# q's shift row in one fp32r matmul: VectorE folds its halves, and the row is summed one tile later

## The chip, the core and the metric

The kernel runs on one core of one Trainium2 chip. The metric is the device time of one execution in microseconds, the median over several executions. The engines are called here as the profile calls them: PE is TensorE's matmuls, PEld its weight loads, DVE is VectorE, ACT is ScalarE, POOL is GpSimd, and SP issues most DMA transfers.

## The reference, cut to what matters

```python
x = A_x                                             # (1, 2048, 448)
mod = (silu(c) @ w_mod).reshape(c.shape[0], 6, 1, -1)
sa, ca, ga, sb, cb, gb = mod[:, 0] ... mod[:, 5]
h = layernorm(x) * (1 + ca) + sa
x = x + ga * A(h)        # linear attention, 16 heads of 28: q, k, v = h @ wqkv, phi(t) = elu(t) + 1
h = layernorm(x) * (1 + cb) + sb
x = x + gb * B(h)        # mixer MLP over the 2048 tokens: gelu(h^T w1 + b1) w2 + b2
```

The change concerns the first step of the attention. For q, and likewise for k, the kernel needs `(layernorm(x) * (1 + ca) + sa) @ w`. It does not normalise x ahead of the projection. It multiplies x itself with `w' = (1 + ca) w` and adds two rank-one terms: minus the token's mean times the column sums of `w'`, and the token's deviation times the *shift row* `sa @ w`. Both rows, the column sums and the shift row, are computed once for q and once for k.

## The kernel before, in words

**Precision.** The products run in fp32r. To keep fp32's precision, a matrix is split into a high part (a copy rounded to fp32r, made by ACT) and a low part (the rest, made by DVE), and a product takes three matmuls: high by high, high by low, low by high. `hh`, `hl` are the high and low parts of x^T, `wh`, `wl` those of `w'` (j = 0 for q, j = 1 for k), `pkh`, `pkl` those of phi(k), `xh`, `xl` those of the normalised x.

**Stages.** First come the projections and the sums over tokens, up to about 100 us. Then come the attention's output and the two layer norms around it, and from about 150 us on the mixer's two large products. Each engine carries out its instructions in the order in which the code writes them (`tc.manual_schedule()`); the engines wait for each other by semaphores. Tiles come from pools: `slots` with 74 buffers, `tok` with 27 (the smaller pool), and `cst` for constants. A new tile gets a buffer that an earlier one has left, and its first writer waits for that one's last user.

**The loop of the change** is `for t in range(4, NT)`: 16 tiles of 128 tokens. In turn t, PE projects k of tile t+1 (`project(t + 1, 1, "kp")`, ten matmuls), closes tile t with the matmul on the two rows (`close(t, 1)`), and adds tile t-4 to the outer product (`a_outer`, eleven matmuls into `cacc`). In odd turns it also transposes the rows of means and deviations of tiles t+1 and t+2 (`a_transpose`, tile `rw`, from `rowst`; ACT copies them into `hl` of both tiles). In turns 10 to 14 it projects one tile of q as well (`a_q`, `qp`). Meanwhile DVE and ACT make phi(k), normalise, split, and prepare two tiles ahead. POOL computes the powers of the variances and issues transfers that add phi(k) into `pkl` and into the running sums `pk0` and `pk1`.

**The shift row of q (j = 0).** In turns 5 to 8, DVE's `row_part` adds up `accb0`: on each of 128 partitions, the four chunks of w_q, each times the column `sa`. What is left to do is to sum over the partitions. In turn 9, behind `close(9, 1)`, PE does seven fp32r matmuls with `sel_s`, which give minus the column sums of `w'` (`row_sum`), and one with `sel_b` on `accb0`, both plain fp32, which gives the shift row (`row_bias`). All go into one PSUM bank, `rowb0`. At the end of turn 9, `row_out` reads the rows out: ACT writes the high parts into `wrow0`, DVE the low parts. The first q tile closes with `wrow0` in turn 10. The same happens for k (j = 1) ahead of the loop, and stays as it is.

**mod.** The shares of w_mod for ga, cb, sb, gb are summed in the same way by `mod_part` (into `acc2`, `acc4`, ...). `mod_add` folds the upper 48 partitions onto the lower, and `mod_high` splits the sum into 64 partitions of high and 64 of low part (`mh`), so that one fp32r matmul with ones (`mod_sum2`, bank `modp`) sums both.

Of the kernel before, what the change touches and what calls it, by code (L numbers as in the profile page):

```python
# [8 lines left out]
F32 = mybir.dt.float32  # L9
F32R = mybir.dt.float32r  # L10
AF = mybir.ActivationFunctionType
# [3 lines left out]
P = 128  # L15
S, D, F = 2048, 448, 1792
# [15 lines left out]
ROWS = 98  # L32
# [19 lines left out]
def block_kernel(ctx: ExitStack, tc: tile.TileContext, x, xt, wqkv, wo, w1, b1, w2, c, wmod, wfirst, out):  # L52
    nc = tc.nc
# [5 lines left out]
    cst = ctx.enter_context(tc.tile_pool(name="cst", bufs=1))  # L59
# [16 lines left out]
    def moving(new, name, dt=F32R, parts=P):  # L76
        return new(name, dt=dt, parts=parts, w=512)[:, 16:16 + D]
# [22 lines left out]
        nc.gpsimd.affine_select(out=m3, in_=m3, compare_op=ALU.is_ge, fill=0.0, base=DH - 1,  # L100
                                pattern=[[0, 4], [DH, 4], [0, DH]], channel_multiplier=-1)

    cst.tile([P, 112], F32, name="space")
    mhalf = cst.tile([P, 2], F32, name="mhalf")
    nc.vector.memset(mhalf, -0.5)
    roots = cst.tile([P, 2], F32, name="roots")
# [2 lines left out]
    sel_b = cst.tile([P, ROWS], F32, name="sel_b")  # L109
# [3 lines left out]
    for i in (64, 66, 96):  # L113
        nc.gpsimd.memset(sel_f[:, i:i + 1], -1.0)
        nc.gpsimd.memset(sel_b[:, i + 1:i + 2], 1.0)
    sel_s = cst.tile([P, ROWS], F32R, name="sel_s")
    rowst = []
    for i in range(RING):
        rowst.append(cst.tile([P, P], F32R, name=f"rowst{i}"))
# [115 lines left out]
    def mod_add(j):  # L235
        acc = macc[j]
        nc.vector.tensor_add(acc[:G - 64], acc[:G - 64], acc[64:])

    def mod_high(j):
        acc, both = macc[j], moving(slot, f"mh{j}")  # L240
        macc[j] = (both,)
        nc.scalar.activation(both[:64], acc[:64], AF.Copy)
        return lambda: nc.vector.tensor_sub(both[64:], acc[:64], both[:64].bitcast(F32))
# [5 lines left out]
    def mod_sum2(j):  # L249
        ps = bank(f"modp{j}")  # L250
        part = macc.pop(j)
        for i, m in enumerate(part):
            nc.tensor.matmul(ps[:, :D], ones_r[:m.shape[0], :], m, start=(i == 0), stop=(i == len(part) - 1))
        return ps

    Whi, Wlo, Wrow, rowb, accb = {}, {}, {}, {}, {}
# [26 lines left out]
    def row_sum(j):  # L283
        rowb[j] = bank(f"rowb{j}")
        ws = [Whi[j, ch] for ch in range(4)] + [Wlo[j, ch] for ch in range(3)]
        for i, w in enumerate(ws):
            nc.tensor.matmul(rowb[j][:ROWS, :D], sel_s, w, start=(i == 0), stop=False)  # L287

    def row_bias(j):
        nc.tensor.matmul(rowb[j][:ROWS, :D], sel_b, accb.pop(j), start=False, stop=True)  # L290

    def row_out(j):
        ps, w = rowb.pop(j), Wrow[j]
        nc.scalar.activation(w[64:ROWS], ps[64:ROWS, :D], AF.Copy)
        nc.vector.tensor_sub(w[96:ROWS], ps[96:ROWS, :D], w[96:ROWS].bitcast(F32))
# [77 lines left out]
    def a_stats_dve(ts):  # L373
        g, ve = a_group(ts)

        b6 = {}

        def first(i):
            b6[i] = small.tile([P, 6], F32, name=f"st{ts[i]}", tag="st")
            nc.vector.bn_stats(b6[i], X[ts[i]])  # L380

        def second(i):
            nc.vector.bn_aggr(mv[ts[i]][:, 0:2], b6[i])

        def end():
            nc.vector.tensor_scalar_add(ve, g[:, :, 1:2].to_broadcast([P, len(ts), 2]), EPS)
            a_pow(g, ve)
            groups[ts[0]] = g
        return first, second, end
# [11 lines left out]
    def a_transpose(t):  # L401
        ps = bank(f"rw{t}")
        tps[t], tps[t + 1] = ps[:ROWS - 64, :P], ps[64:ROWS, :P]
        nc.tensor.transpose(ps[:ROWS, :P], rowst[t // 2 % RING][:, :ROWS].bitcast(F32), ident)
# [29 lines left out]
    def project(t, j, name):  # L434
        projects([(t, kind, ch) for ch in range(3) for kind in ("hh", "wl", "hl")] + [(t, "hh", 3)], j, name)

    def close(t, j):
        ps = pps.pop((t, j))
        nc.tensor.matmul(ps[:, :D], heads[t][1][:ROWS, 384:], Wrow[j][:ROWS], start=False, stop=True)  # L439
        return ps[:, :D]  # L440
# [3 lines left out]
    def a_exp1(t, ps):  # L444
        eks[t] = (slot(f"ek{t}"), slot(f"rk{t}"))
        nc.scalar.activation(eks[t][0], ps, AF.Exp, scale=mv[t][:, 2:3])

    def a_relu(t, ps):
        nc.scalar.activation(eks[t][1], ps, AF.Relu, scale=mv[t][:, 2:3])

    def a_exp(t, ps):
        a_exp1(t, ps)
        a_relu(t, ps)
# [22 lines left out]
    def a_q(t):  # L476
        project(t, 0, "qp")
        qps[t] = close(t, 0)
        del heads[t]
# [30 lines left out]
    def a_pk(t, ps):  # L510
        pkf[t] = phi_k(t, ps, tslot if t < 2 else slot)
# [33 lines left out]
    def a_outer(t):  # L545
        if not cacc:
            cacc.extend(bank(f"cacc{ch}") for ch in range(4))
        xh, xl = xss.pop(t)
        kh, kl = pks.pop(t)
        for ch in range(4):  # L550
            s = slice(ch * P, (ch + 1) * P)
            todo = [(xh, kh), (xh, kl)] + ([(xl, kh)] if ch < 3 else [])
            for i, (a, b) in enumerate(todo[::1 if t > 1 else 2]):
                nc.tensor.matmul(cacc[ch][:, :D], a[:, s], b, start=(t == 0 and i == 0),  # L554
                                 stop=(t == NT - 1 and i == len(todo) - 1))
        if t < 2:
            for ch in range(4):
                nc.tensor.matmul(cacc[ch][:, :D], xh[:, ch * P:(ch + 1) * P], kl, start=False, stop=False)
# [59 lines left out]
    kps = [close(t, 1) for t in (0, 1)]  # L618
# [63 lines left out]
    for t in range(4, NT):  # L682
        if 5 < t < NT - 1:
            project(t + 1, 1, "kp")
        kp = close(t, 1) if t > 4 else kps[4]
        if t == 9:
            row_sum(0)
            row_bias(0)
        if t > 4:
            a_outer(t - KV_LAG)  # L690
        if t % 2 and 4 < t < NT - 2:
            a_transpose(t + 1)
        if t in Q_EARLY:
            a_q(Q_EARLY[t])
        if t == 12:
            mp = mod_sum2(2)
        pair = t % 2 and 7 < t + 3 < NT
        if pair:
            first, second, end = a_stats_dve((t + 3, t + 4))
            first(0)  # L700
        if 5 <= t < 9:
            w_low(0, t - 5)
        if pair:
            second(0)
        if 5 <= t < 9:
            row_part(0, t - 5)
        a_phi_q(t in Q_EARLY)
        if t == 9:
            a_exp(t, kp)
        if t % 2 and 4 < t < NT - 2:  # L710
            a_copy(t + 1)
            a_copy(t + 2)
        if t != 9:
            a_exp(t, kp)
        if 7 < t + 3 < NT:
            a_split_high(t + 3)
        a_pk_parts(t - 1)
        highs = HIGH_AT.get(t, (t - 2,))
        for i in highs[:1]:
            a_norm(i)  # L720
            a_high(i)
        if t % 2 == 0 and 4 < t < NT - 3:
            low = a_rows(t + 2)
        if t == 11:
            low2 = mod_high(2)
        for j, i in MOD_AT.get(t, ()):
            mod_add(j) if i is None else mod_part(j, i)
        if t == 14:
            low4()
        a_pk(t, kp)  # L730
        if t % 2 == 0 and 4 < t < NT - 3:
            low()
        if 7 < t + 3 < NT:
            a_split_low(t + 3)
        for i in highs[1:]:
            a_norm(i)
            a_high(i)
        if pair:
            first(1)
        for i in highs:  # L740
            a_low(i)
        if pair:
            second(1)
            end()
        sum_end()
        if 4 <= t < 8:
            w_high(0, t - 4)
            if t == 7:
                w_row(0)
        if t == 9:  # L750
            row_out(0)
        if t == 12:
            mod_out(2, mp)
            make_mask()
        if t in FETCH:
            load_xt(FETCH[t])
            load_x(FETCH[t])
        if 7 <= t < 11:
            mod_part(2, t - 7)
        if t == 10:  # L760
            mod_add(2)
        if t == 11:
            low2()
        if t == 13:
            low4 = mod_high(4)
        if t in (7, 10):
            load_mod(4 if t == 7 else 3)
        if t == 10:
            load_qkv(2, tslot)
        if t == 8:  # L770
            for g in range(4):
                w = tslot(f"wo{g}", parts=G)
                nc.sync.dma_start(w, wo[g * G:(g + 1) * G, :])
                wo_sb.append(w)
            b12 = cst.tile([P, NF + NT], F32, name="b12")
            nc.sync.dma_start(b12, b1)
            b1c, b2c = b12[:, :NF], b12[:, NF:]
        if t >= 13:
            nc.vector.tensor_mul(wo_sb[t - 13], wo_sb[t - 13], mods[2][:G])
        load_to(PRE_LOAD.get(t, 0))  # L780
# [34 lines left out]
    for ch in range(4):  # L815
        for g in range(4):
            s = slice(g * G, (g + 1) * G)
            nc.tensor.matmul(kvb[:G, s], raw_w[2, ch][:, s], csum[ch][:, s], start=(ch == 0 and g == 0),  # L818
                             stop=(ch == 3), skip_group_check=True)
# [168 lines left out]
    for i in range(NT + LAG):  # L988
# [11 lines left out]
        t = i - LAG  # L1000
# [292 lines left out]
    for o0, n in W1G[1:]:  # L1293
# [5 lines left out]
        for r in range(first, NT):  # L1299
# [5 lines left out]
            if xleft:  # L1305
                t = xleft.pop(0)
# [80 lines left out]
```

## Time and profile before

| | |
|---|---|
| time, median of 3 runs | 433.37 us (433.19 to 434.04) |
| the profiled execution's own time | 434.09 us |
| its span, first to last instruction | 432.4 us |
| granted TensorE clock | 1.0 |
| busy PE, DVE, ACT, POOL | 427.9, 365.1, 278.9, 120.1 us |
| `rowb` matmuls with `sel_s` (L287), for k and q | 14, each 0.36 us from start to end |
| `rowb` matmuls with `sel_b` (L290), for k and q | 4 records, each 0.54 us from start to end |

Matmuls overlap, so that what one of them takes of PE's path is the distance from its start to the next one's, not its duration. The plain fp32 matmul has two records of its own. In rows of the timeline, an entry in brackets at the end is the idle time of that engine before the instruction, and what ended it. An instruction's number of elements is partitions by elements of a partition.

### The profile page before, as it was taken

The page shows a single profiled execution, that of the slowest core. Times are in us where ns is not written, and L with a number is a line of the kernel's source. Part 1 is how long each engine was busy: PE and PEld are TensorE (multiplying, and loading weights), DVE is VectorE, ACT ScalarE, POOL GpSimd, SP SyncE. Part 2 cuts the span into 40 slices and gives each one's busy share as a digit, 9 for nine tenths or more (in the row PEclk, how much of TensorE's full clock was granted, in tenths as well). Part 3 has the DMA queues.
Part 4 walks back from the last instruction along what each step waited for, and adds up shares of the span by engine and source line. Part 5 has one row for each costly group of instructions (what it writes and reads, how often), then busy time and mean ns, then how long its engine had stood idle before and what let it go on. Part 6 is the DMA issues. An engine that isn't in the chain of part 4 may idle for free.

```text
span 432.4 us, 7216 instructions
## 1 busy us (share of the span) xinstructions
PE 427.9 (99%) x2331; PEld 398.0 (92%) x2331; DVE 365.1 (84%) x814; ACT 278.9 (65%) x595; POOL 120.1 (28%) x199
## 2 busy tenths in 40 slices
PE   8999999999999999999999999999999999999997
PEld 8888899999899999999999999999999999999996
DVE  4899987889899999998579695739799998898894
ACT  5799869658578899996755263537464664655550
POOL 4345444300026577775200000010113131132010
PEclk9999999999999999999999999999999999999999
DMA  8997997565300036354427461577379977986431
GB/s 282 385 337 162 239 264 162 89 206 193 86 1 0 26 74 148 74 125 97 145 85 244 142 212 50 166 203 210 79 193 214 207 159 159 214 170 144 85 46 41
DMA packets 63797, 66.14 MB, mean 153 GB/s; under 512 B 4816, under 2 KB 55312, under 8 KB 63760
## 3 DMA queue, kind: packets, MB, share of 16 engines
q1 hardware_dynamic: 54688, 50.90, 37.8%
q0 software_dynamic: 8784, 14.32, 20.8%
q10 hardware_dynamic: 288, 0.46, 0.4%
q8 instruction: 18, 0.29, 0.3%
q14 instruction: 19, 0.16, 0.1%
HBM read 46.30 MB, written 7.34 MB: 124 GB/s over the span
## 4 chain that ended last, share of the span: by engine, by line
PE 97%; DVE 1%; ACT 1%; issue 0%
PE y L1183 19%; PE up L951 10%; PE up L950 10%; PE up L952 10%; PE y L1184 9%; PE cacc L554 7%; PE qp L432 7%; PE op L893 7%; PE kp L432 6%; PE op L900 1%; PE warm L188 1%; PE tq L863 1%; PE qp L439 1%; PE kvb L818 1%; PE wp L968 1%; PE rowb L287 1%
## 5 line engine op out<-in xcount | busy, mean ns | idle before, releaser
L950 PE MATMUL up<-h2h,ph 128*128 128x448 f32 x224 | 81.2, 362 | 0.0
L951 PE MATMUL up<-h2l,ph 128*128 128x448 f32 x224 | 81.2, 362 | 0.0
L952 PE MATMUL up<-h2h,pl 128*128 128x448 f32 x224 | 80.8, 361 | 0.0
L1138 POOL DMA_DIRECT2D a<-a x16 | 14.2, 964 | 142.6 <-DMA pr<-in_B_w_dram 76.7
L950 PEld LDWEIGHTS up<-h2h,ph 128*128 128x128 f32 x224 | 42.0, 188 | 3.1
L952 PEld LDWEIGHTS up<-h2h,pl 128*128 128x128 f32 x224 | 41.9, 187 | 3.0
L951 PEld LDWEIGHTS up<-h2l,ph 128*128 128x128 f32 x224 | 42.0, 188 | 2.3
L84 DVE TENSOR_TENSOR pl<-pr,ph 128x512 fp32r<-128x512 f32 x46 | 30.7, 688 | 2.6 <-ACT ph L83 1.7
L1189 ACT ACTIVATE cc<-y 128x448 f32<-128x448 f32 x24 | 13.0, 546 | 26.7 <-PE y L1184 26.7
L1102 DVE TENSOR_TENSOR u<-u,mod 128x448 f32<-128x448 f32 x14 | 8.7, 623 | 23.0 <-ACT u L1101 22.8
L83 ACT ACTIVATE ph<-pr 128x512 fp32r<-128x512 f32 x46 | 27.6, 623 | 0.8 <-PE up L952 0.5
L1101 ACT ACTIVATE u<-up,b 128x448 f32<-128x448 f32 x14 | 8.8, 625 | 25.4 <-PE up L952 24.9
L432 PE MATMUL kp<-wh,hh 128*128 128x448 f32 x64 | 23.8, 377 | 0.0
L554 PE MATMUL cacc<-pkh,xh 128*128 128x448 f32 x64 | 23.6, 369 | 0.0
L432 PE MATMUL qp<-wh,hh 128*128 128x448 f32 x64 | 23.5, 368 | 0.0
L1203 POOL DMA_DIRECT2D out_dram<-yt x14 | 12.7, 909 | 37.3 <-DVE yt L1194 27.9
L843 POOL TENSOR_SCALAR den<-den 128x16 f32<-128x16 f32 x16 | 8.8, 548 | 44.2 <-DVE den L840 44.2
L554 PE MATMUL cacc<-pkl,xh 128*128 128x448 f32 x56 | 20.3, 362 | 0.0
L893 PE MATMUL op<-wph,pth 128*128 128x448 f32 x48 | 18.7, 390 | 0.0
L1144 DVE TENSOR_TENSOR a<-a,s 128x512 f32<-128x512 f32 (+1 forms) x32 | 18.5, 622 | 0.0
L83 ACT ACTIVATE s2h<-s 128x512 fp32r<-128x512 f32 (+1 forms) x16 | 8.3, 569 | 15.5 <-DVE s L1144 15.5
L1183 PE MATMUL y<-ub,a11h 128*128 128x448 f32 x56 | 18.2, 375 | 0.0
(235 smaller groups left out, 1383.7 us busy)
## 6 DMA issues: line engine op xcount, KB each, us to landing
pr<-in_B_w_dram SPq DMA_DIRECT2D x56, 256.0 KB, 3.1
a<-in_B_w_dram SPq DMA_DIRECT2D x32, 256.0 KB, 4.8
a<-in_B_w_dram SPq DMA_DIRECT2D x32, 192.0 KB, 4.7
xt<-in_xt_dram SPq DMA_DIRECT2D x16, 256.0 KB, 5.0
x<-in_A_x_dram SPq DMA_DIRECT2D x16, 224.0 KB, 5.0
wm<-in_B_wmod_dram SPq DMA_DIRECT2D x16, 196.0 KB, 5.2
out_dram<-x SPq DMA_DIRECT2D x14, 224.0 KB, 2.3
out_dram<-yt POOLq DMA_DIRECT2D x14, 224.0 KB, 6.1
```

What stands on the lines that cost most here:

```text
L83: nc.scalar.activation(hi, full, AF.Copy)
L84: nc.vector.tensor_sub(lo, full, hi.bitcast(F32))
L432: nc.tensor.matmul(pps[t, j][:, :D], a[:, ch * P:(ch + 1) * P], w, start=first, stop=False)
L554: nc.tensor.matmul(cacc[ch][:, :D], a[:, s], b, start=(t == 0 and i == 0), stop=(t == NT - 1 and i == len(todo) - 1))
L893: nc.tensor.matmul(opb[t][:, :D], a, b, start=(ch == n == 0), stop=False)
L950: nc.tensor.matmul(ps[:, :D], hi[:, sl], mh, start=first, stop=False)
L951: nc.tensor.matmul(ps[:, :D], hi[:, sl], ml, start=False, stop=False)
L952: nc.tensor.matmul(ps[:, :D], lo[:, sl], mh, start=False, stop=last)
L1138: nc.gpsimd.dma_start(w, a, accum_op=ALU.add)
L1144: nc.vector.tensor_tensor(w, raw2[q, a][i], raw2[q, b][i], op=op)
L1183: nc.tensor.matmul(ps[:, :D], h[:, s], w, start=opens and r == 0, stop=False, skip_group_check=True)
L1184: nc.tensor.matmul(ps[:, :HD], l[:, s], wh, start=False, stop=closes and r == PAIRS - 1, skip_group_check=True)
```

## The change

For q alone, the shift row goes the way of the mod shares:

- In turn 8, behind the low part of the rows of tiles 10 and 11, DVE folds the upper half of `accb0` onto the lower (`row_fold`).
- In turn 9, ACT writes the high part of the 64 partitions into a new tile `rb0` of the smaller pool, and a copy of `sel_b` in fp32r, `sel_r`; DVE writes the low part into `rb0`'s other 64 partitions (`row_high`).
- `row_sum` and `row_bias` move from turn 9 to turn 10, behind tile 11's projection. `row_bias` is now one fp32r matmul of `sel_r` on `rb0`.
- `row_out` moves from the end of turn 9 to turn 10, behind `close(10, 1)`.
- `a_exp(9)` comes ahead of the statistics in turn 9.
- `mod_add(2)` moves from the end of turn 10 into turn 11, ahead of `mod_high(2)`.
- A constant that only took up space shrinks by as much as `sel_r` takes.

```diff
-    cst.tile([P, 112], F32, name="space")
+    cst.tile([P, 14], F32, name="space")
...
+    sel_r = cst.tile([P, ROWS], F32R, name="sel_r")
...
     def row_bias(j):
-        nc.tensor.matmul(rowb[j][:ROWS, :D], sel_b, accb.pop(j), start=False, stop=True)
+        nc.tensor.matmul(rowb[j][:ROWS, :D], sel_r if j == 0 else sel_b, accb.pop(j), start=False, stop=True)
+
+    def row_fold(j):
+        acc = accb[j]
+        nc.vector.tensor_add(acc[:64], acc[:64], acc[64:])
+
+    def row_high(j):
+        acc, both = accb[j], moving(tslot, f"rb{j}")
+        nc.scalar.activation(both[:64], acc[:64], AF.Copy)
+        nc.scalar.activation(sel_r, sel_b, AF.Copy)
+        accb[j] = both
+        return lambda: nc.vector.tensor_sub(both[64:], acc[:64], both[:64].bitcast(F32))
...
         if 5 < t < NT - 1:
             project(t + 1, 1, "kp")
-        kp = close(t, 1) if t > 4 else kps[4]
-        if t == 9:
+        if t == 10:
             row_sum(0)
             row_bias(0)
+        kp = close(t, 1) if t > 4 else kps[4]
+        if t == 10:
+            row_out(0)
         if t > 4:
             a_outer(t - KV_LAG)
...
+        if t == 9:
+            a_exp(t, kp)
+            row_high(0)()
         if pair:
             first, second, end = a_stats_dve((t + 3, t + 4))
             first(0)
...
         a_phi_q(t in Q_EARLY)
-        if t == 9:
-            a_exp(t, kp)
...
         if t == 11:
+            mod_add(2)
             low2 = mod_high(2)
...
         if t % 2 == 0 and 4 < t < NT - 3:
             low()
+        if t == 8:
+            row_fold(0)
...
-        if t == 9:
-            row_out(0)
...
-        if t == 10:
-            mod_add(2)
```

The order on PE around turns 9 and 10. Before, behind the closing matmul of tile 9 (the ellipses leave out the row's other matmuls and those of the outer product and the projection):

```order
L439 MATMUL kp9_733<-wrow1_280,hl9_630 128x448
L287 MATMUL rowb0_806<-wh0_0_534,sel_s_100 98x448
...
L290 MATMUL rowb0_806<-accb0_561,sel_b_90 98x448
L554 MATMUL cacc0_437<-pkh5_632,xh5_701 128x448
...
L404 MATMUL rw10_826<-ident_78,rowst2_105 98x128
L432 MATMUL kp11_870<-wh1_0_222,hh11_762 128x448
L432 MATMUL kp11_870<-wl1_0_224,hh11_762 128x448
L432 MATMUL kp11_870<-wh1_0_222,hl11_763 128x448
...
L439 MATMUL kp10_794<-wrow1_280,hl10_692 128x448
```

And now:

```order
L451 MATMUL kp9_734<-wrow1_281,hl9_631 128x448
L566 MATMUL cacc0_438<-pkh5_633,xh5_702 128x448
...
L416 MATMUL rw10_819<-ident_78,rowst2_106 98x128
L444 MATMUL kp11_865<-wh1_0_223,hh11_763 128x448
L444 MATMUL kp11_865<-wl1_0_225,hh11_763 128x448
L444 MATMUL kp11_865<-wh1_0_223,hl11_764 128x448
...
L288 MATMUL rowb0_876<-wh0_0_535,sel_s_100 98x448
...
L291 MATMUL rowb0_876<-rb0_825,sel_r_101 98x448
L451 MATMUL kp10_796<-wrow1_281,hl10_693 128x448
```

The eight matmuls of the row moved behind the outer product of tile 5, the rows of tiles 10 and 11 and the projection of tile 11.

The order on DVE in turns 8 and 9, with the semaphores that an instruction waits for in brackets (`DMAHW` those of SP's transfers, `DMASW` those of POOL's). Before:

```order
L395 CAST rowst2_105<-mv10_677 128x4x2 [waits Pool_49]
L458 SCALAR_TENSOR_TENSOR pk8_776<-ek8_758,rk8_759 128x448 [waits Activation_49]
L398 TENSOR_TENSOR rowst2_105<-mv10_677,rowst2_105 128x2x2 [waits DVE_49]
L415 TENSOR_TENSOR hl11_763<-xt11_536,hh11_762 128x512 [waits DMAHW3_49,Activation_49]
L505 TENSOR_TENSOR xh6_772<-xn6_770,xh6_772 128x64 [waits DMASW6_49,DMASW5_49,Activation_49]
L506 TENSOR_TENSOR xl6_773<-xn6_770,xh6_772 128x384
L232 SCALAR_TENSOR_TENSOR acc2_723<-wm2_1_374,sc_194,acc2_723 112x448 [waits DMAHW6_49]
L380 BN_STATS st12_830<-x12_597 128x6 [waits DMAHW6_49]
```

And now:

```order
L407 CAST rowst2_106<-mv10_678 128x4x2 [waits Pool_49]
L470 SCALAR_TENSOR_TENSOR pk8_777<-ek8_759,rk8_760 128x448 [waits Activation_49]
L410 TENSOR_TENSOR rowst2_106<-mv10_678,rowst2_106 128x2x2 [waits DVE_49]
L295 TENSOR_TENSOR accb0_562<-accb0_562 64x448
L427 TENSOR_TENSOR hl11_764<-xt11_537,hh11_763 128x512 [waits DMAHW3_49,DVE_49,Activation_49]
L517 TENSOR_TENSOR xh6_773<-xn6_771,xh6_773 128x64 [waits DMASW6_49,DMASW5_49,Activation_49]
L518 TENSOR_TENSOR xl6_774<-xn6_771,xh6_773 128x384
L233 SCALAR_TENSOR_TENSOR acc2_724<-wm2_1_375,sc_195,acc2_724 112x448 [waits DMAHW6_49]
L302 TENSOR_TENSOR rb0_825<-accb0_562,rb0_825 64x448 [waits Activation_49]
L392 BN_STATS st12_831<-x12_598 128x6 [waits DMAHW6_49]
```

The fold stands between the rows' low part and hl11, and hl11 has a wait for a semaphore of DVE's own beside the two that it had; rb0's low part follows four instructions on, ahead of the statistics of x12.

The order on DVE in turn 11, around the first writers that wait for the buffer of pk9 (phi(k) of tile 9). Before:

```order
L496 TENSOR_SCALAR xn9_1014<-x9_370,mv8_554 128x448
L230 TENSOR_SCALAR acc4_1021<-wm4_0_725,sc_194 112x448 [waits DMAHW1_49,PE_49]
L232 SCALAR_TENSOR_TENSOR acc4_1021<-wm4_1_727,sc_194,acc4_1021 112x448 [waits DMAHW2_49,DVE_49]
L232 SCALAR_TENSOR_TENSOR acc4_1021<-wm4_2_729,sc_194,acc4_1021 112x448 [waits DVE_49]
L458 SCALAR_TENSOR_TENSOR pk11_1025<-ek11_1002,rk11_1003 128x448 [waits PE_49,Activation_49]
L415 TENSOR_TENSOR hl14_1007<-xt14_865,hh14_1006 128x512 [waits DMAHW2_49,Activation_49]
L380 BN_STATS st15_1028<-x15_932 128x6 [waits DMAHW5_49]
L505 TENSOR_TENSOR xh9_1016<-xn9_1014,xh9_1016 128x64 [waits DMASW6_49,DMASW5_49,Activation_49]
L506 TENSOR_TENSOR xl9_1017<-xn9_1014,xh9_1016 128x384
```

And now:

```order
L508 TENSOR_SCALAR xn9_1019<-x9_371,mv8_555 128x448
L238 TENSOR_TENSOR acc2_724<-acc2_724 48x448
L231 TENSOR_SCALAR acc4_1027<-wm4_0_726,sc_195 112x448 [waits DMASW6_49,DMAHW1_49,DMASW5_49,DVE_49]
L233 SCALAR_TENSOR_TENSOR acc4_1027<-wm4_1_728,sc_195,acc4_1027 112x448 [waits DMAHW2_49,DVE_49]
L233 SCALAR_TENSOR_TENSOR acc4_1027<-wm4_2_730,sc_195,acc4_1027 112x448 [waits DVE_49]
L470 SCALAR_TENSOR_TENSOR pk11_1031<-ek11_1007,rk11_1008 128x448 [waits PE_49,Activation_49]
L427 TENSOR_TENSOR hl14_1012<-xt14_860,hh14_1011 128x512 [waits DMAHW2_49,Activation_49]
L392 BN_STATS st15_1034<-x15_938 128x6 [waits DMAHW5_49]
L517 TENSOR_TENSOR xh9_1021<-xn9_1019,xh9_1021 128x64 [waits Activation_49]
```

`mod_add(2)` (the 48-partition add on `acc2`) came in front of acc4, and the wait for POOL's two transfers out of pk9 moved from xh9 to acc4's first instruction, six instructions sooner. ACT's high part of x9 (`L500`), which also waited for them, does no more. mh2's low part, for `mod_sum2(2)`, follows three or four instructions behind the last row shown.

## The prediction

> **What bounds the kernel now.** I read the page's busy times and clock first, then the chain that ended last, then who waited for whom on TensorE, and last the timelines of TensorE, VectorE and ScalarE between 38 and 75 us, where all of the change lies.
>
> ```profile
> span 432.4 us, 7216 instructions
> PE 427.9 (99%) x2331; PEld 398.0 (92%) x2331; DVE 365.1 (84%) x814; ACT 278.9 (65%) x595; POOL 120.1 (28%) x199
> PEclk9999999999999999999999999999999999999999
> PE 97%; DVE 1%; ACT 1%; issue 0%
> ...
> PEld kp L432 <- DVE hl L415: 0.8, 4, 0.3
> PEld cacc L554 <- DVE xl L506: 0.5, 1, 0.5
> ```
>
> TensorE is the bound: 97% of the chain, at a granted clock that is full in every slice. So a microsecond taken from TensorE is a microsecond of the kernel, and one in which TensorE waits is a microsecond lost. The last two rows are the only waits that matter here: TensorE's weight loads (PEld, which hold the stationary tile) waited five times for a low part that VectorE had just made. VectorE is the engine close behind TensorE in this stage, and the change gives VectorE two more instructions there while it brings TensorE to VectorE's results sooner.
>
> **The change part by part.** The four rows of the chain of waits around q's shift row in tile 9:
>
> ```profile
> 49.06 1.42 PE rowb L287 x7
> 50.48 0.75 PE rowb L290 x2
> 51.23 2.22 PE cacc L554 x11
> 53.45 0.11 PE rw L404
> ```
>
> *The matmul.* The fp32 bias matmul (two records, 0.75 us of path) becomes one in fp32r. Its nearest rows are the seven in the line above, same 98 rows out and same 448 columns: 1.42 / 7 = 0.20 us each. Gain: 0.75 - 0.20 = 0.55 us of TensorE. That is all that the change can take off the path.
>
> *The move.* These 1.42 + 0.75 = 2.17 us stood ahead of tile 5's outer product, tile 10's transposed rows and tile 11's projection. Now all three come 2.17 us earlier, and the row's eight matmuls come behind them. What each of them needs:
>
> ```profile
> 50.64 0.16 DVE L398 TENSOR_TENSOR rowst<-mv,rowst 128x4 fp32r<-128x4 f32 x1
> 50.71 0.69 DVE L415 TENSOR_TENSOR hl<-xt,hh 128x512 fp32r<-128x512 f32 x1
> 42.01 0.86 POOL L528 DMA_DIRECT2D pkl<-pk  x1 [0.17 <-issue]
> DMA to landing us min/median/max: 3.2/4.0/6.5
> 53.09 0.13 PEld L404 LDWEIGHTS rw<-ident,rowst 128*98 128x98 f32 x1
> 53.61 0.19 PEld L432 LDWEIGHTS kp<-wh,hl 128*128 128x128 f32 x1
> ```
>
> The outer product needs pkl5, which POOL sends off at 42.01; by the longest landing of that kind it is there at 48.5, and the product starts at 51.23 - 2.17 = 49.06: no wait, 0.6 us spare. The transpose's weight load moves from 53.09 to 50.92 and needs rowst2, ready at 50.64 + 0.16 = 50.80, in front of the fold: just in time. The first weight load of hl11 moves from 53.61 to 51.44, and hl11 was ready at 50.71 + 0.69 = 51.40 before. But the fold now stands right in front of hl11 on VectorE.
>
> *The fold.* Its nearest row is the other such add, of 48 partitions, with what precedes and follows it:
>
> ```profile
> 61.00 0.68 DVE L232 SCALAR_TENSOR_TENSOR acc<-wm,sc,acc 112x448 f32<-112x448 f32 x1
> 61.72 0.62 DVE L237 TENSOR_TENSOR acc<-acc 48x448 f32<-48x448 f32 x1
> 62.26 0.62 DVE L380 BATCH_NORM_STATS2 st<-x 128x6 f32<-128x448 f32 x1
> ```
>
> It lasts 0.62 us. It began 0.04 behind the end of the instruction before it (61.68); the one after it began 0.08 before its own end. In the changed order hl11 has a wait on VectorE itself that it did not have, so hl11 too begins 0.04 behind the fold's end. With both gaps: fold 50.84 to 51.46, hl11 51.50 to 52.19. With neither (the least): the fold at 50.71, hl11 0.54 later, done at 51.94.
>
> How a late low part costs TensorE is shown once in nearly this size, where xl0 was late:
>
> ```profile
> 30.11 0.55 DVE L506 TENSOR_TENSOR xl<-xn,xh 128x384 fp32r<-128x384 f32 x1
> 30.22 0.37 PE L554 MATMUL cacc<-pkh,xh 128*128 128x448 f32 x1
> 30.71 0.19 PEld L554 LDWEIGHTS cacc<-pkh,xl 128*128 128x128 f32 x1 [0.51 <-DVE xl L506]
> 31.02 0.37 PE L554 MATMUL cacc<-pkh,xh 128*128 128x448 f32 x1
> ```
>
> The load came 0.05 behind the end of xl (30.66). It was due with the matmul before it, at 30.22, so it was 0.49 late; the next matmul but one was due at 30.62 and came at 31.02, so TensorE lost 0.40, or 0.09 less than the load's delay. For hl11: load at 52.19 + 0.05 = 52.24, due at 51.44, 0.80 late, loss 0.71 us. With the least: 0.55 late, loss 0.46. So the move costs between 0.46 and 0.71, against a gain of 0.55. I take 0.71, since the two gaps of the nearest row apply to a fold that reads from partitions 0 and 64 and to an hl11 that waits.
>
> [...]
>
> *ScalarE's two instructions.* ScalarE has room in tile 9:
>
> ```profile
> 51.15 0.63 ACT L449 ACTIVATE rk<-kp,mv 128x448 f32<-128x448 f32 x1
> 53.59 0.57 ACT L407 ACTIVATE hl<-rw 34x128 fp32r<-34x128 f32 x2 [1.82 <-PE rw L404]
> 55.41 0.37 PE L439 MATMUL kp<-wrow,hl 98*128 98x448 f32 x1
> 54.85 0.69 DVE L415 TENSOR_TENSOR hl<-xt,hh 128x512 fp32r<-128x512 f32 x1 [0.56 <-ACT hh L411]
> 56.40 0.23 DVE L505 TENSOR_TENSOR xh<-xn,xh 128x64 fp32r<-128x64 f32 x1 [0.32 <-ACT xh L500]
> L242 ACT ACTIVATE mh<-acc x4: 562/564/566, 68.9 to 203.0; 64x448 fp32r<-64x448 f32 x4
> ```
>
> rb0's high part (0.56, as the L242 row has for the same shape) and sel_r (98 columns, so less than half of that) run from 51.78 to about 52.6, inside the 1.82 us that ScalarE waited for TensorE. Then it copies hl10, which tile 10's closing matmul (55.41 before) wants only at 55.57. Free, and ScalarE is about 1 us ahead afterwards. If that cover were gone it would cost ScalarE the 0.8 us itself, still ahead of that matmul.
>
> *The low part of rb0 on VectorE* (0.62, and held at both ends as L243 is below) ends at about 54.1. TensorE wants it at the row's last matmul, 0.20 ahead of the closing one, at 55.37: 1.2 us spare. VectorE is then about 1.4 us behind its old times, but it used to idle 0.56 and 0.32 us for ScalarE behind hl12 and xh7, which ScalarE now has ready; about 0.5 stays until mod_add(2), another add of 0.62, is missing at the end of tile 10. Behind its new place, ScalarE's high part of mh2 now waits for it; that add ends at about 64.6, and ScalarE came to mh2 at 68.9 (the L242 row's first).
>
> *wrow0.* Read out at the same place of ScalarE's queue, and one instruction later in VectorE's:
>
> ```profile
> 56.39 0.54 ACT L294 ACTIVATE wrow<-rowb 34x448 fp32r<-34x448 f32 x1
> 57.42 0.63 DVE L295 TENSOR_TENSOR wrow<-rowb,wrow 2x448 fp32r<-2x448 f32 x1
> 59.83 0.36 PE L439 MATMUL qp<-wrow,hl 98*128 98x448 f32 x1
> ```
>
> ScalarE's copy can start when the row is summed, about 55.8 (0.36 us behind its last matmul's start). VectorE's part ends at about 59.2, and the first q tile closes at 59.83 + 0.16: 0.7 us spare, no cost.
>
> *mod_add(2) and the buffers.* The changed program hands buffers out in another turn. acc4 gets the one of pk9, so VectorE's first acc4 instruction waits for POOL's two transfers out of pk9. Before, ScalarE's xh9 had that wait:
>
> ```profile
> 61.01 0.86 POOL L541 DMA_DIRECT2D pk<-pk  x1
> 64.44 0.45 DVE L230 TENSOR_SCALAR acc<-wm,sc 112x448 f32<-112x448 f32 x1 [0.40 <-PE cacc L554]
> 64.93 1.41 DVE L232 SCALAR_TENSOR_TENSOR acc<-wm,sc,acc 112x448 f32<-112x448 f32 x2
> 66.54 0.62 DVE L458 SCALAR_TENSOR_TENSOR pk<-ek,rk 128x448 f32<-128x448 f32 x1 [0.20 <-ACT rk L449]
> 68.43 0.58 ACT L500 ACTIVATE xh<-xn 128x448 fp32r<-128x448 f32 x1 [0.32 <-DMA pk<-pk]
> 69.04 0.23 DVE L505 TENSOR_TENSOR xh<-xn,xh 128x64 fp32r<-128x64 f32 x1 [0.73 <-ACT xh L500]
> 70.06 0.62 DVE L243 TENSOR_TENSOR mh<-acc,mh 64x448 fp32r<-64x448 f32 x1
> 73.43 0.36 PE L253 MATMUL modp<-mh,ones_r 128*128 128x448 f32 x1
> ```
>
> VectorE will stand idle from about 64.6 to 68.4. Behind it in its queue are acc4's other two, pk11, hl14, xh9, xl9 and mh2; the first that TensorE wants is mh2, at 73.43 + 0.16 = 73.59. From acc4's start to pk11's is 1.82 us (64.44 to 66.34, less 0.08), from pk11's to mh2's end 4.14, of which 0.73 was the wait for xh9, which is gone: 68.43 + 1.82 + 3.41 + 0.05 = 73.71. That costs 0.12 us at most. POOL issues that transfer up to 0.5 us sooner now, since ScalarE's pkl9 comes sooner, so I count 0 and keep 0.12 for the range. Everything else behind the idle time has over 2 us: tile 14's projection and its rows come at 73.6 and 78.
>
> *The sum*: -0.55 + 0.71 = +0.16 us. The profiled execution took 434.09 (span 432.4 and 1.7 around it), so this one would have taken 434.25. It is the slowest end of its three runs; their median is 433.37, and with +0.16 I forecast 433.5. Run to run the three differ by 0.2%, and 0.2% (0.87 us) is about what a measurement of this kernel can tell from no change.
>
> **The rivals.**
>
> (1) *The gain shows*: the fold finds room and hl11 is not late, so 433.37 - 0.55 = 432.8. For it: VectorE need run only 0.8 us sooner against TensorE for hl11 to be in time. Against it: nothing ahead of the fold changes on VectorE, and TensorE's arrival is fixed by the chain. Still within 0.2%.
>
> (2) *Slower, by the transfer out of pk9*: it decides from a start of acc4 at 73.59 - (1.82 + 3.41 + 0.05) = 68.31 on, and each microsecond beyond that is one of the kernel, through mh2 and the matmul on it. At 69.0 the total passes 0.87 us, 434.2. For it: that transfer was issued at 61.01 and awaited until 68.43, over the loads of w_mod and w_qkv that tile 10 sends off. Against it: it is issued sooner, and x14 and xt14, whose loads wait for tile 5's outer product, go 2 us sooner, out of its way.
>
> (3) *The matmul stays at 0.75* since its operands are still 4 bytes wide: then +0.71, 434.1. Against it: the seven rows of L287.
>
> **How the numbers follow.** Forecast (hl11 late by about what the matmul saves, -0.1 to +0.3 us): 0.70. Rival 1: 0.18. Rival 2: 0.06, half of it over 0.2%. Rival 3: 0.03. Something that I don't see: 0.03. All but half of rival 2, the unseen and the scatter of medians lie within 0.2%: same 0.87, slower 0.07, faster 0.06. The range takes rival 1 at its low end and rival 2's lower half at its high end, with 0.1 for the scatter: 432.7 to 434.0.
>
> **What would show it.** Right: in the chain the row's eight matmuls take 1.62 us; the load of hl11 waits about 0.7 us for VectorE at 51.5 to 52.3; tile 10's closing matmul starts at 55.41 + 0.16; acc4 on VectorE waits for a DMA until about 68; wrow0 is waited for by nobody on TensorE. Wrong: hl11's load comes within 0.2 us of 51.44 (rival 1), or the matmul on mh2 waits over 0.5 us (rival 2).

## The result and the profile after

The changed kernel takes 437.31 us, median of 6 runs (436.03 to 438.95), against 434.15 (433.19 to 434.36, 6 runs) before: 1.008 of the time, 95% interval 1.0065 to 1.0094. It is slower by 3.2 us by the two medians (3.5 by the ratio), where 433.5 was forecast with a range up to 434.0. The profiled execution took 437.45.

The page's head:

```profile
span 435.7 us, 7218 instructions
PE 430.6 (99%) x2330; PEld 397.9 (91%) x2330; DVE 366.1 (84%) x816; ACT 279.9 (64%) x597; POOL 120.3 (28%) x199
PEclk9999999999999999999999999999999999999999
```

From the list of TensorE's waits the rows that are new or have grown (us in total, times, longest):

```profile
PEld kp L444 <- DVE hl L427: 1.5, 5, 0.7
PEld modp L254 <- issue: 0.8, 1, 0.8
```

The clock is full in every slice, as before. PE's busy time has grown by 2.7 us, with one record fewer: its matmuls have become longer. The waits of the weight loads have grown by 0.7 us for hl (L427) and 0.8 us for the matmul on mh2 (L254).

The chain of waits around tile 11's projection (start, us, what):

```profile
50.93 0.62 DVE accb L295
51.55 0.09 issue
51.64 0.70 DVE hl L427
52.34 0.04 issue
52.38 1.91 PE kp L444 x8
54.29 1.41 PE rowb L288 x7
55.71 0.20 PE rowb L291
```

The timeline there, and around the matmul on mh2:

```profile
52.38 0.19 PEld L444 LDWEIGHTS kp<-wh,hl 128*128 128x128 f32 x1 [0.73 <-DVE hl L427]
...
60.63 1.55 POOL L553 DMA_DIRECT2D pk<-pk  x1
...
64.04 0.62 DVE L238 TENSOR_TENSOR acc<-acc 48x448 f32<-48x448 f32 x1
69.19 0.56 DVE L231 TENSOR_SCALAR acc<-wm,sc 112x448 f32<-112x448 f32 x1 [4.53 <-DMA pk<-pk]
...
73.78 0.62 DVE L244 TENSOR_TENSOR mh<-acc,mh 64x448 fp32r<-64x448 f32 x1
...
74.55 0.44 PE L254 MATMUL modp<-mh,ones_r 128*128 128x448 f32 x1 [0.40 <-DVE mh L244]
```

Both waits of the prediction are there: hl11 stands behind the fold, and acc4 (L231) waits for the transfer out of pk9's buffer, so that mh2 comes at 74.40 and TensorE waits for it. But these two do not make up the loss: by the table at the end of this section, 2.2 of 3.2 us go behind 74 us, where TensorE has no new wait. The rows of one line, with minimum, median and maximum of the durations in ns, before (L432) and after (L444):

```profile
L432 PEld LDWEIGHTS qp<-wl,hh x48: 187/188/192, 57.8 to 141.5; 128*128 128x128 f32 x48
L432 PE MATMUL qp<-wl,hh x48: 360/363/368, 58.0 to 141.7; 128*128 128x448 f32 x48
```

```profile
L444 PEld LDWEIGHTS qp<-wl,hh x48: 187/188/192, 58.2 to 143.6; 128*128 128x128 f32 x48
L444 PE MATMUL qp<-wl,hh x48: 360/367/370, 58.4 to 143.8; 128*128 128x448 f32 x48
```

The weight load is as long as before, the matmul 4 ns longer. The distance from start to start has grown by as much, as rows of the chain around 90 to 100 us show, where TensorE waits for nothing; before, and after:

```profile
87.41 11.01 PE cacc L554 x55
98.82 2.00 PE qp L432 x10
```

```profile
88.77 11.02 PE cacc L566 x55
100.18 2.05 PE qp L444 x10
```

Ten matmuls of a q projection take 2.05 us in place of 2.00, and 55 of the outer product 11.0 us as before. The projections stream tiles of the smaller pool (wh, wl), the outer product tiles of the larger one (pkh, pkl).

How far a matmul comes behind the same matmul of before, by the two timelines of TensorE, in us, for the changed kernel and the runs below. The profiled executions differ by up to 0.6 us by the time the change begins, so each row is to be read from column to column:

| kernel | tile 10's projection (46.90) | closing tile 10 (55.41) | the one behind mh2's (73.63) | q projection (98.86) | MLP (299.90) | near the end (424.94) |
|---|---|---|---|---|---|---|
| changed | +0.18 | +0.34 | +1.20 | +1.36 | +2.88 | +3.38 |
| e1_aligned | -0.54 | -0.36 | +0.39 | +0.37 | +0.37 | +0.37 |
| e2_before_shifted | -0.61 | -0.51 | -0.29 | -0.14 | +1.38 | +1.88 |
| g1_acc4_small_pool | -0.22 | -0.05 | -0.04 | -0.05 | -0.05 | -0.04 |
| f1_fold_behind_hl11 | -0.02 | -0.57 | -0.19 | -0.26 | -0.26 | -0.25 |
| h1_fold_behind_acc4_small | -0.12 | -0.68 | -0.70 | -0.75 | -0.75 | -0.75 |

The changed kernel loses time all the way, also after 75 us, where the change has no instruction.

### The profile page after: what moved, and what is told of

It reads as the page before. It is cut to its first block, busy times and chain, and to the rows that moved or that the text cites. A ratio compares the mean times of both kernels' runs of the same rounds, so it can differ in the third digit from the quotient of the medians.

```text
span 435.7 us, 7218 instructions
## 1 busy us (share of the span) xinstructions
PE 430.6 (99%) x2330; PEld 397.9 (91%) x2330; DVE 366.1 (84%) x816; ACT 279.9 (64%) x597; POOL 120.3 (28%) x199
## 4 chain that ended last, share of the span: by engine, by line
PE 85%; ACT 1%; DVE 1%; issue 0%; ACTq 0%
PE y L1197 19%; PE up L964 10%; PE up L966 10%; PE up L965 10%; PE y L1198 9%; PE op L907 7%; PE qp L444 7%; PE cacc L566 5%; PE kp L444 2%; PE op L914 2%; PE tq L877 1%; PE kvb L832 1%; PE wp L982 1%; PE qp L451 1%; PE y L1194 0%; PE rowb L288 0%
## 5 line engine op out<-in xcount | busy, mean ns | idle before, releaser
L444 PE MATMUL kp<-wh,hh 128*128 128x448 f32 x64 | 24.1, 381 | 0.0
L444 PE MATMUL qp<-wh,hh 128*128 128x448 f32 x64 | 23.8, 373 | 0.0
```

The lines of the kernel that those rows point to most:

```text
L444: nc.tensor.matmul(pps[t, j][:, :D], a[:, ch * P:(ch + 1) * P], w, start=first, stop=False)
```

## The experiments

**The addresses.** Theory A: the diff's first line moved the smaller pool. The program lays tiles out in steps of 32 bytes; `space` and `sel_r` now take 64 + 416 bytes in place of 448, and every tile of that pool starts 32 bytes later (wh0_0 at 203424 in place of 203392). The rival, B: the new order makes the engines collide.

```diff
 changed kernel, e1_aligned:
-    cst.tile([P, 14], F32, name="space")
+    cst.tile([P, 8], F32, name="space")
 kernel before, e2_before_shifted:
-    cst.tile([P, 112], F32, name="space")
+    cst.tile([P, 120], F32, name="space")
```

> The changed kernel with the constant "space" at 8 floats in place of 14. The program lays tiles out in steps of 32 bytes, so 14 floats and the 98 of sel_r take 64 + 416 = 480 bytes where the 112 of before took 448: in the changed kernel every tile of the smaller pool (wh, wl, wrow, wph, wpl) starts 32 bytes later. With 8 floats they stand where they stood before; nothing else changes. Theory A (address): the matmuls that stream these tiles took about 205 ns from start to start after the change and 200.5 before, some 550 of them, 2.5 us; with the old addresses they are back at 200.5 to 201 and about 0.6 us over before is left (hl11's wait and that of the matmul on mh2, less the saved pass): 1.001 of before. Theory B (order): the matmuls are slower because the new order makes the engines collide; then the time stays at 1.008 of before.

> The kernel before with "space" at 120 floats in place of 112, so that the smaller pool's tiles start 32 bytes later and nothing else changes. Theory A (address): each of the some 550 matmuls that stream a tile of that pool takes 205 ns in place of 200.5, 2.5 to 2.9 us in all, 1.006 to 1.007 of before. Theory B (order): the same time as before, 1.000.

Measured: e1_aligned 434.96 us (434.05 to 436.52), 1.004 of before (1.0027 to 1.0053), so 2.35 us less than the changed kernel; e2_before_shifted 435.94 (435.76 to 436.36), 1.0057 (1.0045 to 1.007), 2.50 us more than the 433.44 of the runs of before beside it. In the table, e1's row stays level behind 73.63, and e2's climbs by 2.5 us (-0.61 to +1.88) without any change of order. Theory A holds, and B falls for this part. e1 is still 1.5 us behind, not the 0.6 expected, and its runs scatter more than those of before: a second loss of changing size is left, which the runs after these go into.

**Which address counts.** Here the streamed tiles' first column is moved inside their buffers (it is column 16 in the kernel), and once the larger pool as a whole:

```diff
 kernel before, e3_offsets (e5_offsets2 in brackets):
-    def moving(new, name, dt=F32R, parts=P):
-        return new(name, dt=dt, parts=parts, w=512)[:, 16:16 + D]
+    def moving(new, name, dt=F32R, parts=P, at=16):
+        return new(name, dt=dt, parts=parts, w=512)[:, at:at + D]
 # q's wh, wl, wrow at=0 (28); k's at=8 (12); wph, wpl at=4 (2); pkh, pkl at=24 (18); h2h, h2l at=20 (32)
 kernel before, e4_large_pool_shifted:
+    pre.tile([P, 8], F32, name="pre")      # in front of the larger pool
-    cst.tile([P, 112], F32, name="space")
+    cst.tile([P, 104], F32, name="space")
```

> The kernel before, with the first column of the streamed tiles moved inside their buffers, by another amount for each family: against a multiple of 128 bytes the streamed rows start at 0 for q's weights, 32 for k's, 16 for the output projection's, 96 for the pk parts and 80 for the MLP's first matmuls (64 for all of them before). Theory A, if what counts is a multiple of 64 bytes: q's stays at 200.5 ns from start to start, all other four families go to about 205. If what counts is 64 exactly, q's goes up too. If it is only the parity of 32 bytes, k's and the pk parts go up and 16 and 80 may go either way. Theory B: no family changes, all within 1 ns of before.

> The kernel before with the larger pool 32 bytes later and the smaller pool where it was (8 floats in front, "space" 8 floats shorter). Now the stationary tiles of the k and q projections start 32 bytes off and their streamed tiles do not; for the outer products and the MLP's first matmuls both are off. Theory A with the streamed operand alone: k and q stay at 200.5 to 201 ns, the outer products and the MLP's first matmuls (200.0 on average before) go to about 204.5, 180 and 672 of them, 3.8 us in all. If the stationary operand's address counts as well, k and q go up too. Theory B: nothing changes.

> The kernel before with the streamed tiles' first column moved again: against a multiple of 128 bytes the rows start at 112 for q's weights, 48 for k's, 8 for the output projection's, 72 for the pk parts, 0 for the MLP's first matmuls; the stationary tiles stay at 0. The runs so far gave for the distance between streamed and stationary rows: 64 bytes 200.3 ns from start to start; 96 and 32 about 205; 80 203.2; 0 203.8; 16 202.2; and with the stationary tiles moved by 32 as well (distance 64) 200.3 again. If the distance modulo 128 decides, with its lowest cost at 64, then 72 costs under 203, 48 and 112 between 202 and 205, 0 again 203 to 204 although another family has it, 8 between 202 and 204. If only the streamed address decides by multiples of 64, 0 gives 200.3 and all others 205.

One run each: 437.25, 435.17 and 439.30 us. The mean distance from start to start of neighbouring matmuls with the same output, worked out from TensorE's timeline (110 to 160 pairs in a family, 659 for the MLP; in brackets the start of the streamed row less that of the stationary one, modulo 128 bytes, for most of the family):

| kernel | k | q | output projection | outer product | MLP, first matmuls |
|---|---|---|---|---|---|
| before | 200.7 (64) | 200.3 (64) | 200.4 (64) | 201.0 (64) | 200.0 (64) |
| changed | 205.4 (96) | 205.0 (96) | 205.2 (96) | 201.0 (64) | 200.4 (64) |
| e1_aligned | 201.0 (64) | 200.0 (64) | 200.3 (64) | 200.6 (64) | 200.0 (64) |
| e2_before_shifted | 204.8 (96) | 205.2 (96) | 205.2 (96) | 200.6 (64) | 200.4 (64) |
| e3_offsets | 205.0 (32) | 203.8 (0) | 202.2 (16) | 205.2 (96) | 203.2 (80) |
| e4_large_pool_shifted | 204.9 (32) | 205.9 (32) | 205.0 (32) | 200.3 (64) | 200.3 (64) |
| e5_offsets2 | 203.0 (48) | 206.2 (112) | 204.0 (8) | 206.8 (72) | 204.1 (0) |

Rows of the chain of e4_large_pool_shifted, at the place of those above:

```profile
87.28 11.01 PE cacc L556 x55
98.68 2.07 PE qp L434 x10
```

This was a miss for theory A in its first form. In e4 the streamed tiles of q stand where they stood, only the stationary ones (hh, hl) have moved, and ten matmuls take 2.07 us in place of 2.00. In the outer product both have moved, and it takes 11.01 us as before. So it is not the streamed operand's address alone, and its distance from the stationary one's fits every run; the stationary rows stood at only two places, 0 and 32. At a distance of 64 bytes (modulo 128) a matmul takes 200 to 201 ns; at each of the nine other distances that were run it takes 202 to 207. A multiple of 64 does not do: 0 costs 4 ns. Nor is there one valley around 64, as I had expected: 72 gave 206.8 in place of less than 203, and 112 gave 206.2 in place of at most 205. The form of this curve stays open, and so does what in the chip makes it.

The changed kernel shows the same inside one family. Of the MLP's weight pieces only three lie in the smaller pool (`TOKP`, pieces 9 to 11), as stationary tiles, so they moved and their streamed tiles did not. Their 36 matmuls now come 206 ns apart on average, the other 636 of the first product 200 to 201; before, all of them came about 200 apart. The MLP's second product, which the table leaves out, lost 0.5 us in the changed kernel and in e2 (the two last columns of the earlier table); which of its tiles make it was not worked out.

**The second loss: who gets pk9's buffer.** All of these stand on e1_aligned:

```diff
 f1_fold_behind_hl11, from e1_aligned:
-        if t == 8:
-            row_fold(0)
         if 7 < t + 3 < NT:
             a_split_low(t + 3)
+        if t == 8:
+            row_fold(0)
 g1_acc4_small_pool, from e1_aligned:
-            macc[j] = (tslot if j == 5 else slot)(f"acc{j}", parts=G)
+            macc[j] = (tslot if j > 3 else slot)(f"acc{j}", parts=G)
 h1_fold_behind_acc4_small: both
```

> The changed kernel with the old addresses ("space" 8), the fold where the change put it, and acc4 in a buffer of the smaller pool, which has nothing to wait for; xn11 then takes another buffer too. Theory A: the wait at the matmul on mh2 goes, with it the scatter; hl11's wait stays: +0.16 us, 1.0004 of before (433.6). Theory B (mh2 is late through mod_add's later place, not through acc4's buffer): the matmul on mh2 waits as before, 1.004.

Measured: 433.59 us (433.07 to 434.35), 1.0000 (0.9991 to 1.0008). The matmul on mh2 no longer waits (the table's row stays at -0.05), 1.4 us of e1's median are gone, and so is its scatter. (In its profiled execution, 0.5 us below its median, e1 lost 0.75 us there.) pk9's buffer now went to pk11, which waited until later than acc4 in the changed kernel, but mh2 was ready at 72.78, in time. Rows of VectorE's timeline:

```profile
64.34 0.45 DVE L231 TENSOR_SCALAR acc<-wm,sc 112x448 f32<-112x448 f32 x1
64.83 1.41 DVE L233 SCALAR_TENSOR_TENSOR acc<-wm,sc,acc 112x448 f32<-112x448 f32 x2
69.47 0.63 DVE L470 SCALAR_TENSOR_TENSOR pk<-ek,rk 128x448 f32<-128x448 f32 x1 [3.24 <-DMA pk<-pk]
...
72.16 0.62 DVE L244 TENSOR_TENSOR mh<-acc,mh 64x448 fp32r<-64x448 f32 x1
```

Theory B, that mod_add's later place makes mh2 late, falls: it has that place here too. What is left is hl11's wait, and it comes out as +0.17 us between the columns 46.90 and 55.41, in this run as in e1 (+0.18).

> The changed kernel with the old addresses ("space" 8), and the fold issued behind hl11's subtraction in place of in front of it. That also changes the hand-out of buffers: acc4 takes xh7's, as before the change, and no longer waits for POOL's transfer out of pk9. In the run with the old addresses alone TensorE was 0.17 us behind its old times once tile 10's closing matmul was reached, and another 0.67 us behind it at the matmul on mh2. Theory A (hl11's wait, and acc4's wait for pk9's buffer, are all that is left): both go, the saved pass shows, -0.55 us: 432.9, 0.9987 of before, and the scatter of the runs (434.05 to 436.52) shrinks to that of before. Theory B (the row's new place or the work added to VectorE and ScalarE costs by itself): 1.002 to 1.004 stays.

Measured: 433.34 us (432.93 to 434.00), 0.9995 (0.9986 to 1.0004). hl11 is in time, and TensorE gains 0.55 us up to the closing of tile 10 (-0.02 to -0.57): the whole of the saved pass. But 0.38 us of it is lost again at mh2. The expectation was wrong in that acc4 was only the first to have that buffer; now hl14 has it:

```profile
67.05 0.63 DVE L470 SCALAR_TENSOR_TENSOR pk<-ek,rk 128x448 f32<-128x448 f32 x1 [0.52 <-ACT rk L461]
70.24 0.69 DVE L427 TENSOR_TENSOR hl<-xt,hh 128x512 fp32r<-128x512 f32 x1 [2.56 <-DMA pk<-pk]
...
72.40 0.62 DVE L244 TENSOR_TENSOR mh<-acc,mh 64x448 fp32r<-64x448 f32 x1
```

> The changed kernel with the old addresses, the fold behind hl11 and acc4 in the smaller pool. With the fold behind hl11 alone TensorE was 0.57 us ahead of its old times at tile 10's closing matmul, and 0.27 at the matmul on mh2: hl14 had taken pk9's buffer, VectorE stood 2.56 us for the transfer out of it, and mh2 came late. Here xl9 takes that buffer, which is the last but three of VectorE's instructions ahead of mh2; the transfer may land as late as 70.2, as it did there, and mh2 is still ready near 72, before 72.9. Theory A: the whole of the saved pass stays, -0.55 us, 432.85, 0.9987 of before. Theory B (mh2 is late for other reasons, or the gain is lost behind it): 0.9995 as with the fold behind hl11 alone.

Measured: 433.30 us (432.74 to 433.71), 0.9991 (0.9982 to 1.0000), against 433.46 before. In the trace the gain stays: from -0.12 ahead of the change to -0.68 at the closing of tile 10, -0.70 behind mh2 and -0.75 at the end, with mh2 made from 69.55 on. The median is 0.16 better, not 0.55; the interval holds 0.9987, and it reaches 1.0000. So this version is not slower than either kernel, and by its trace 0.6 us faster than the one before; by its times that is hardly told from no change, and where the rest of the 0.55 is was not found.

**The fold's gap.** f4_fold_same_partitions, from e1_aligned:

```diff
-        nc.vector.tensor_add(acc[:64], acc[:64], acc[64:])
+        nc.vector.tensor_add(acc[:64], acc[:64], acc[:64])
```

> The changed kernel with the old addresses, and a fold that adds partitions 0 to 63 of accb to themselves; the sum of the upper 64 partitions is left out. Same size, but both inputs start at partition 0. If the fold is held for a second input that starts in another quarter of the partitions, it now starts 0.08 us in front of the end of rowst2's last row instruction, where it began 0.04 behind it, and hl11 comes 0.12 sooner. If it is held for something else (its result's place, a wait on VectorE itself), it starts 0.04 behind that end again.

434.71 us, one run. Rows of VectorE's timeline in e1_aligned, and in this run:

```profile
50.08 0.15 DVE L410 TENSOR_TENSOR rowst<-mv,rowst 128x4 fp32r<-128x4 f32 x1
50.26 0.62 DVE L295 TENSOR_TENSOR accb<-accb 64x448 f32<-64x448 f32 x1
50.97 0.69 DVE L427 TENSOR_TENSOR hl<-xt,hh 128x512 fp32r<-128x512 f32 x1
```

```profile
50.09 0.16 DVE L410 TENSOR_TENSOR rowst<-mv,rowst 128x4 fp32r<-128x4 f32 x1
50.16 0.61 DVE L295 TENSOR_TENSOR accb<-accb 64x448 f32<-64x448 f32 x1
50.70 0.68 DVE L427 TENSOR_TENSOR hl<-xt,hh 128x512 fp32r<-128x512 f32 x1
```

With inputs from partitions 0 and 64 the fold began 0.03 us behind the end of rowst2's instruction, with both from 0 it began 0.09 in front of it. So in these two traces the fold's gap goes with the place of its second input. Only the starts 0 and 64 were run; for which other places an instruction is held, and why, was not shown. hl11 came 0.27 us sooner, not 0.12: its own wait for the fold, with which it began 0.09 behind the fold's end, is also gone from the program here, and it began 0.07 in front of it.

**The move alone.** m1_move_alone, from the kernel before: `row_sum(0)`, `row_bias(0)` and `row_out(0)` moved as in the change, nothing added.

> The kernel before with q's shift row moved and nothing else: its eight matmuls (the last still the two passes of fp32) stand behind tile 11's projection ahead of tile 10's closing matmul, its reading out behind that. No fold, no rb0, mod_add(2) and all buffers as before. Theory A: the move by itself costs and gains nothing, since hl11, pkl5 and rowst2 are just in time for a TensorE that comes 2.17 us sooner: 433.4, 1.000 of before. Theory B (hl11's first load, due at 51.44 with hl11 ready at 51.40, is late even without the fold): up to +0.1 us, 1.0002; a time of 1.001 or more would mean that the move itself costs.

Measured: 434.04 us (433.28 to 434.90), 1.0013 (1.0003 to 1.0023), a miss. The move costs nothing at its own place: the outer product behind tile 10's closing matmul starts 0.59 us ahead of the old times, as did tile 10's projection (0.58). But 0.44 us is lost again at 64.3, and the expectation's "all buffers as before" was false. ScalarE's second reading of the q tile (L466) has got a buffer that a transfer still reads, and TensorE waits for the bank that it empties; from there on it is 0.15 us ahead:

```profile
59.62 0.63 ACT L465 ACTIVATE eq<-qp,mv 128x448 f32<-128x448 f32 x1 [0.82 <-PE qp L439]
63.63 0.64 ACT L466 ACTIVATE rq<-qp,mv 128x448 f32<-128x448 f32 x1 [3.38 <-DMA pk<-pk]
...
64.32 0.19 PEld L432 LDWEIGHTS qp<-wh,hh 128*128 128x128 f32 x1 [0.56 <-ACT rq L466]
```

## Why the prediction was wrong, by its steps

- *The matmul, -0.55 us.* Right. The row's eight matmuls took 1.41 + 0.20 = 1.61 us (1.62 forecast), and f1 shows -0.55 by itself. Rival 3 falls. With the addresses as before and acc4 out of pk9's buffer (g1) the kernel took 433.59, where 433.5 was forecast: this term and the next were the ones that the forecast was made of.
- *hl11's wait, +0.71 us.* Right. With the old addresses its net effect with the step above was +0.17 and +0.18 (+0.16 forecast), so the wait costs 0.72. Wrong in it is the gap: hl11 began 0.09 behind the fold, not 0.04.
- *ScalarE, the low part of rb0, wrow0.* Right: ScalarE's two instructions lay at 51.80 to 52.54, and nobody on TensorE waited for rb0, sel_r or wrow0.
- *acc4 and pk9's buffer, counted 0, at most 0.12.* The mechanism was right and is rival 2, to which I gave 0.06. The mis-sized term is the transfer's landing. I took 68.43 from a single execution and argued that it could only come sooner. POOL did issue it sooner, at 60.63 in place of 61.01, but the instruction that waited for it began 8.56 us later, at 69.19, in place of 7.42. It began at 69.47, 70.24 and 68.67 in g1, f1 and h1, in g1 and h1 9.20 and 8.29 us behind the issue; why the transfer takes longer there stays open. From 69.19, the prediction's 5.28 us to mh2's use give 74.47, and the load came at 74.52; it was due at 73.78, so 0.74 late, and the matmul behind mh2's began 0.65 late. That is the 0.09 less that was read from xl0's row. The 0.12 was too small even for a landing at 68.43: it set the load's time (73.71) against that of the matmul, where the load was due 0.20 sooner, and the rule used for hl11 gives 0.23. Over the runs, e1 less g1, it costs 1.4 us and makes the scatter.
- *`space`.* This is the step that failed, with 2.35 to 2.50 us. It has no place in the prediction, so it was costed at nothing without a word, and the text ahead of it says that the constant shrinks by as much as `sel_r` takes. That holds in floats (98) and not in bytes as laid out (384 less, 416 more). Nothing in the profile of before shows what an address costs, since the five families of the table all stand at the same distance; but the kernel starts its streamed tiles at column 16 and carries a tile that nobody reads, and both asked for a rival of their own.

Together, by the medians: -0.55 + 0.72 + 1.4 + 2.35 = 3.9 us, against 437.31 - 433.4 = 3.9 (3.2 by the 434.15 of the runs of before beside it). The last two terms are differences between the same medians, so this sum had to close. The traces are the check: there mh2 cost 0.65 and the moved pool alone 2.49 (e2, from -0.61 to +1.88), and -0.55 + 0.72 + 0.65 + 2.49 = 3.3, against 3.2 (from +0.18 to +3.38) in the changed kernel.

## What to carry to other kernels

When a diff adds, drops or resizes a tile, work out where everything behind it now lies before costing any instruction: in e2_before_shifted a constant longer by 32 bytes took the matmuls that stream from the pool behind it from 200 to 205 ns. Where pools hand buffers out in order, an instruction put in front of another changes who waits for whose last user; find the one that has got the buffer with the slow reader, ask what stands behind it on its engine, and don't take a transfer's landing from one execution (the first instruction to wait for the one out of pk9's buffer began at 68.43 us before, at 69.19 in the changed kernel and at 70.24 in f1). The gain of 0.55 us on the bound engine is real in f1's trace, and 0.38 of it is gone again, since one such wait moved onto the path.

## What was unexpected of the hardware

In these runs the time of a 448-column fp32r matmul with a weight load of its own, from start to start, went with the distance between the starts of its two operands' rows: 200 to 201 ns at 64 bytes modulo 128, 202 to 207 at 0, 8, 16, 32, 48, 72, 80, 96 and 112. The weight loads of the q and k projections kept a median duration of 187 to 188 ns at 0, 32, 64 and 96. In the changed kernel it shows in no wait, and the busy share stays at 99%; for q it shows only in a median duration of 367 in place of 363 ns, and in a stretch of ten matmuls of 2.05 in place of 2.00 us.
